# Reading w2 in whole 14 KiB runs in a DMA-bound decode kernel

## The chip, the cores and the metric

The kernel runs on one core of one Trainium2 chip. The metric is the device time of one execution in microseconds (us). Beside it each run lists the span of the core, from its first to its last instruction; the device time is longer than the span by some 2 us ("beyond the span" means device time minus span).

The names in the profiles: PE multiplies matrices (PEld loads its weights), DVE and ACT are the vector and the scalar engine, SP issues the large loads. A DMA is one such load; 16 DMA engines share its work. A load has landed when its last data have arrived in the on-chip memory. HBM is the large memory beside the chip's cores. A run of 14 KiB is a contiguous stretch of memory; a run of a kernel is one execution.

## The reference

One decode step for a batch of 4 with one token each, D = 1024. It is a pre-norm attention block with 32 query heads over 4 key/value heads (only the last 2048 of 8192 cached positions are used), followed by a gated feed-forward block with F = 3584, both with residuals. What matters here is its last line:

```python
gate = einsum("bsd,df->bsf", x, w1); up = einsum("bsd,df->bsf", x, w3)
h = silu(gate) * up
out = einsum("bsf,fd->bsd", h, w2)          # w2: (3584, 1024) bf16
```

With so few tokens the work is to read 55.6 MB of weights and caches once. w2 is 7.3 MB of that and is read last.

## The kernel before

All large loads go through one ring of ten buffers and are issued from SP in the order in which they are used: wq, k, v, wo, w1, w3, w2. Each is a chunk of about 2 MB. w2 is cut into JG = 4 chunks; in a chunk each of the 128 partitions takes IF = 7 consecutive rows of 2 KiB, 14 KiB that are contiguous in HBM.

```python
stream = ctx.enter_context(tc.tile_pool(name="stream", bufs=10))
w2_v = B_w2.rearrange("(j p i) n -> p j i n", p=P, i=IF)

def load_w2(j, pieces):
    w2_t = stream.tile([P, IF, D], BF16, tag="s")
    i = 0
    for n in pieces:                        # rows per DMA
        nc.sync.dma_start(out=w2_t[:, i : i + n, :], in_=w2_v[:, j, i : i + n, :])
        i += n
    return w2_t

plan = (
    # ... wq, k, v, wo, w1, w3 ...
    + [("w2", load_w2, (j, [4, 3] if j < JG - 1 else [3, 2, 1, 1])) for j in range(JG)]
)
```

The matmuls of a piece can start when its DMA has landed: four for each row i, one per quarter of the output columns.

```python
for jf in range(JG):
    w2_t = loaded["w2"][jf]
    for i in range(IF):
        for j in range(JG):
            nc.tensor.matmul(y2_ps[QD * j : QD * j + B, :], lhsT=hgT[:, i, jf, :],
                             rhs=w2_t[:, i, j * CG : (j + 1) * CG],
                             start=False, stop=(jf == JG - 1 and i == IF - 1),
                             skip_group_check=True)

res = act.tile([P, CG], BF16)
nc.vector.tensor_copy(out=res[:, : CG // 2], in_=y2_ps[:, : CG // 2])
nc.scalar.copy(out=res[:, CG // 2 :], in_=y2_ps[:, CG // 2 :])
# ... four small DMAs of res to the output, two on SP and two on ACT ...
```

## Time and profile before

| | before |
|---|---|
| device time, median of 3 runs | 140.01 us (139.9 to 140.39) |
| span of the profiled run | 138.2 us |
| data moved | 55.74 MB in 7025 DMA packets, 403 GB/s |
| busy: DMA engines / PE / DVE / ACT | 90% or more in slices 2 to 38 of 40 / 54% / 27% / 21% |

These are lines of the page of before: the engines' busy time and share of the span, the DMA engines' busy tenths and GB/s in 40 equal slices, the packets, and the shares of the chain that ended last.

```profile
span 138.2 us, 2365 instructions
PE 75.0 (54%) x1057; PEld 43.4 (31%) x1057; DVE 37.1 (27%) x71; ACT 29.4 (21%) x29; POOL 0.7 (1%) x6
...
DMA  5999999999999999999999999999999999999950
GB/s 154 433 423 436 417 436 436 441 413 432 441 402 409 420 421 416 425 423 430 429 429 417 425 442 424 428 432 428 432 428 432 432 432 413 421 427 430 409 216 2
DMA packets 7025, 55.74 MB, mean 403 GB/s; under 512 B 580, under 2 KB 612, under 8 KB 3560
...
DMA 74%; PE 16%; ACT 5%; SPq 1%; issue 1%; DVE 0%; ACTq 0%
```

The row of nines is the main reading: from the first microseconds to the last piece of w2 the DMA engines are busy 90% of the time or more, and no compute engine is busy for more than 54%. PE waits in the chain of k look like time (PE 16%), but the stream runs on below them.

The end of the same chain in order of time (start, duration, what) shows what stands behind the last landing:

```profile
121.33 12.97 DMA w_t<-in_B_w_dram
134.29 0.04 issue
134.34 0.41 PE y_ps L448 x4
134.75 0.02 issue
134.77 0.30 DVE res L458
135.07 0.02 issue
135.10 0.27 ACT res L459
```

Only four matmuls, two casts and the output DMA. The timeline of the w2 stage on PE (start, duration, engine, line, operation, count, and in brackets the idle time before it and what ended it):

```profile
121.20 1.66 PE L448 MATMUL y_ps<-w_t,hgT 128*4 128x256 bf16 x28 [0.31 <-DVE hgT L439]
123.84 1.02 PE L448 MATMUL y_ps<-w_t,hgT 128*4 128x256 bf16 x16 [0.97 <-DMA w_t<-in_B_w_dram]
...
125.68 0.81 PE L448 MATMUL y_ps<-w_t,hgT 128*4 128x256 bf16 x12 [0.82 <-DMA w_t<-in_B_w_dram]
...
128.11 1.02 PE L448 MATMUL y_ps<-w_t,hgT 128*4 128x256 bf16 x16 [1.61 <-DMA w_t<-in_B_w_dram]
...
133.08 1.00 PE L448 MATMUL y_ps<-w_t,hgT 128*4 128x256 bf16 x12 [0.42 <-DMA w_t<-in_B_w_dram]
...
134.34 0.38 PE L448 MATMUL y_ps<-w_t,hgT 128*4 128x256 bf16 x4 [0.25 <-DMA w_t<-in_B_w_dram]
```

PE is idle before every piece, and from the second chunk on the DMA ends the idle each time; before the first chunk, at 121.20 us, PE waited 0.31 us for DVE's copy of the transposed operand. The pieces come as the loads were cut: 16 and 12 matmuls for 4 and 3 rows. The tile view gives the issue times of the ten w2 DMAs on SP (count, duration in ns, first and last start in us):

```profile
L130 SPq DMA_DIRECT2D w_t<-in_B_w_dram x10: 328/328/328, 87.4 to 121.3; - x10
```

The last one is issued 13 us ahead of its landing.

Two readings come from the trace's packet records, one record for each packet. First, the duration of a packet by its size:

```
size     2 KiB   4 KiB   6 KiB   8 KiB   14 KiB   16 KiB   4 B (completion)
ns          84     159     234     309      535      611     9
```

That is 9 ns plus 37.6 ns per KiB (the prediction below says 36.6, a slip on which nothing else rests). Second, the 4-byte completion packets that each DMA engine writes at the end of its share show how the engines advance: 4.26 us per chunk of w1 or w3 (14 KiB runs), 4.30 to 4.31 us per chunk of w2. The bytes are the same.

### The profile page before, as it was taken

To read this page: it belongs to the slowest core of one execution; us is meant where nothing else is said; L and a number is where in the kernel's file an instruction comes from. 1 tells how busy PE (TensorE), PEld (TensorE's weight loads), DVE (VectorE), ACT (ScalarE), POOL (GpSimd) and SP (SyncE) were. 2 spreads that over 40 slices of the span, in tenths; PEclk is the share of its full clock that TensorE was granted. 3 is DMA by queue.
4 is the path that set the end of the run, shared out by engine and by line. 5 is a ranking of instruction groups with operands and counts; after the bars stand their busy time and mean duration, and the time that the engine had idled before them with its cause. 6 is when DMAs were issued, how large, how long until landed. Compare 5 with 4: busy or idle time off the path is not lost.

```text
span 138.2 us, 2365 instructions
## 1 busy us (share of the span) xinstructions
PE 75.0 (54%) x1057; PEld 43.4 (31%) x1057; DVE 37.1 (27%) x71; ACT 29.4 (21%) x29; POOL 0.7 (1%) x6
## 2 busy tenths in 40 slices
PE   0152254499798989300795489383244432663560
PEld 0111011295656556000795356131011110231220
DVE  6610000244343434520500460600008930300000
ACT  1200000126464646279420000000051000000000
POOL 2000000000000000000000000000000000000000
PEclk9999999999999999955555556855555555555555
DMA  5999999999999999999999999999999999999950
GB/s 154 433 423 436 417 436 436 441 413 432 441 402 409 420 421 416 425 423 430 429 429 417 425 442 424 428 432 428 432 428 432 432 432 413 421 427 430 409 216 2
DMA packets 7025, 55.74 MB, mean 403 GB/s; under 512 B 580, under 2 KB 612, under 8 KB 3560
## 3 DMA queue, kind: packets, MB, share of 16 engines
q1 hardware_dynamic: 6960, 55.58, 95.7%
q8 instruction: 8, 0.13, 0.3%
q10 hardware_dynamic: 56, 0.02, 0.1%
q14 instruction: 1, 0.01, 0.0%
HBM read 55.59 MB, written 0.01 MB: 402 GB/s over the span
## 4 chain that ended last, share of the span: by engine, by line
DMA 74%; PE 16%; ACT 5%; SPq 1%; issue 1%; DVE 0%; ACTq 0%
DMA w_t<-in_B_w_dram 55%; DMA k_t<-in_A_k_cache_dram 14%; PE kt_ps L271 10%; DMA wq_t<-in_A_wq_dram 5%; ACT kT L277 5%; PE scores_ps L256 5%; SPq L118 1%; PE y_ps L448 0%; DVE res L458 0%; ACT res L459 0%; SPq L111 0%; ACTq L277 0%
## 5 line engine op out<-in xcount | busy, mean ns | idle before, releaser
L277 ACT COPY kT<-kt_ps 128x1024 bf16<-128x1024 bf16 x16 | 15.9, 1013 | 14.5 <-PE kt_ps L271 14.5
L271 PE MATMUL kt_ps<-ident,k_t 128*128 128x128 bf16 x256 | 18.0, 231 | 0.9 <-DMA k_t<-in_A_k_cache_dram 0.9
L271 PEld LDWEIGHTS <-k_t 128*128 128x128 bf16 x256 | 15.9, 104 | 6.1 <-issue 4.9
L275 DVE COPY kT<-kt_ps 128x1024 bf16<-128x1024 bf16 x16 | 11.1, 692 | 17.6 <-PE kt_ps L271 17.6
L223 PE MATMUL q_ps<-wq_t,xnT 128*4 128x512 bf16 x64 | 7.5, 620 | 11.2 <-DMA wq_t<-in_A_wq_dram 11.2
L414 PE MATMUL u_ps<-w_t,hnT 128*4 128x448 bf16 x64 | 6.7, 567 | 10.3 <-DMA w_t<-in_B_w_dram 10.3
L256 PE MATMUL scores_ps<-kT,qz 128*32 128x512 bf16 x64 | 9.9, 609 | 3.0 <-ACT kT L277 3.0
L414 PEld LDWEIGHTS <-hnT 128*4 128x4 bf16 x128 | 3.9, 109 | 24.0 <-issue 23.4
L448 PE MATMUL y_ps<-w_t,hgT 128*4 128x256 bf16 x112 | 7.5, 404 | 6.3 <-DMA w_t<-in_B_w_dram 6.0
L414 PE MATMUL g_ps<-w_t,hnT 128*4 128x448 bf16 x64 | 6.5, 570 | 5.0 <-DMA w_t<-in_B_w_dram 4.7
L323 PE MATMUL OT_ps<-PT_sb,v_t 128*128 128x8 bf16 x256 | 7.4, 168 | 1.7 <-issue 1.4
L323 PEld LDWEIGHTS <-v_t 128*128 128x128 bf16 x256 | 7.3, 104 | 1.9 <-issue 1.7
L359 PE MATMUL y_ps<-wo_t,o_954 128*4 128x256 bf16 x128 | 6.4, 391 | 1.7 <-DVE y_ps L349 1.7
L223 PEld LDWEIGHTS <-xnT 128*4 128x4 bf16 x64 | 2.0, 106 | 15.8 <-issue 15.5
L309 PE MATMUL pt_ps<-Dm,Pm 128*128 128x128 bf16 x16 | 1.9, 308 | 9.3 <-DVE Dm L302 9.3
L459 ACT CAST res<-y_ps 128x128 bf16<-128x128 f32 x1 | 0.3, 267 | 31.0 <-DVE res L458 31.0
L448 PEld LDWEIGHTS <-hgT 128*4 128x4 bf16 x112 | 3.5, 103 | 10.3 <-issue 8.4
L427 DVE RECIPROCAL eg<-eg 128x896 f32<-128x896 f32 x1 | 5.8, 5753 | 0.0
L359 PEld LDWEIGHTS <-o_954 128*4 128x4 bf16 x128 | 4.0, 119 | 4.1 <-DVE y_ps L349 2.0
L233 DVE TENSOR_SCALAR q_sb<-q_ps 128x512 bf16<-128x512 f32 x1 | 0.7, 693 | 16.9 <-PE q_ps L223 16.9
L234 ACT ACTIVATE q_sb<-q_ps 128x512 bf16<-128x512 f32 x1 | 0.6, 597 | 20.9 <-DVE q_sb L233 20.9
L295 ACT ACTIVATE Pm<-scores_ps,nmax 128x2048 bf16<-128x2048 f32 x1 | 4.8, 4784 | 0.0
(73 smaller groups left out, 40.7 us busy)
## 6 DMA issues: line engine op xcount, KB each, us to landing
w_t<-in_B_w_dram SPq DMA_DIRECT2D x8, 1792.0 KB, 33.2
wq_t<-in_A_wq_dram SPq DMA_DIRECT2D x4, 2048.0 KB, 11.6
k_t<-in_A_k_cache_dram SPq DMA_DIRECT2D x4, 2048.0 KB
v_t<-in_A_v_cache_dram SPq DMA_DIRECT2D x4, 2048.0 KB, 40.4
wo_t<-in_A_wo_dram SPq DMA_DIRECT2D x4, 2048.0 KB
w_t<-in_B_w_dram SPq DMA_DIRECT2D x3, 1024.0 KB
w_t<-in_B_w_dram SPq DMA_DIRECT2D x4, 768.0 KB, 29.7
w_t<-in_B_w_dram SPq DMA_DIRECT2D x1, 512.0 KB
```

The costliest lines, as they stand in the source:

```text
L223: nc.tensor.matmul(q_ps[QD * g : QD * g + B, hf * 512 : (hf + 1) * 512], lhsT=xnT[:, kc, :], rhs=wq_t[:, kc % KPC, c0 : c0 + 512], start=( ...
L256: nc.tensor.matmul(scores_ps[QD * g : QD * (g + 1), n * 512 : (n + 1) * 512], lhsT=qz[:, b, g * QD : (g + 1) * QD], rhs=kT_v[:, g, :, :], ...
L271: nc.tensor.transpose(out=kt_ps[:, jj, :], in_=k_v[:, n * NJ + t * TB + jj, :], identity=ident[:])
L275: nc.vector.tensor_copy(out=kT[:, t * TB : (t + 1) * TB, :], in_=kt_ps[:])
L277: nc.scalar.copy(out=kT[:, t * TB : (t + 1) * TB, :], in_=kt_ps[:])
L295: nc.scalar.activation(out=Pm[:].rearrange("q (c jq) -> q jq c", jq=NSB), in_=scores_ps[:].rearrange("q (jq c) -> q jq c", jq=NSB), func=A ...
L309: nc.tensor.matmul(pt_ps[:, jj, :], lhsT=Pm[:, (jb * JPB + jj) * P : (jb * JPB + jj + 1) * P], rhs=Dm[:], start=True, stop=True)
L323: nc.tensor.matmul(OT_ps[:, b, g * REP : (g + 1) * REP], lhsT=v_t[:, g, j, :], rhs=PT_sb[:, j, g * QD + b * REP : g * QD + (b + 1) * REP], ...
L359: nc.tensor.matmul(y_ps[QD * j : QD * j + B, :], lhsT=o4[:, h4, r, :], rhs=wo_t[:, h4 % (HPC // RPO), r, j * CG : (j + 1) * CG], start=(h4 ...
L414: nc.tensor.matmul(out_ps[QD * j : QD * j + B, hf, :HF], lhsT=hnT[:, k2, r, :], rhs=w_t[:, r, c0 : c0 + HF], start=(k2 == 0 and r == 0), s ...
L427: nc.vector.reciprocal(out=eg[:], in_=eg[:])
L448: nc.tensor.matmul(y2_ps[QD * j : QD * j + B, :], lhsT=hgT[:, i, jf, :], rhs=w2_t[:, i, j * CG : (j + 1) * CG], start=False, stop=(jf == J ...
```

## The change

The intent is to spend fewer DMA packets and fewer DMAs on w2. The first three chunks are read in one DMA each, a 14 KiB run per partition. The last is cut into 4, 2 and 1 rows instead of 3, 2, 1 and 1.

```diff
-        + [("w2", load_w2, (j, [4, 3] if j < JG - 1 else [3, 2, 1, 1])) for j in range(JG)]
+        + [("w2", load_w2, (j, [IF] if j < JG - 1 else [4, 2, 1])) for j in range(JG)]
```

## The prediction

> **What bounds the kernel now.** The DMA stream. The profile page shows the 16 DMA engines 90% busy or more in slices 2 to 38 of 40, at 402 to 442 GB/s, while PE is busy 54% of the span, DVE 27%, ACT 21%. The chain of waits is 74% DMA and ends in three waits for w2 landings, the last at 134.29 us; after it stand only four matmuls (0.41 us), two casts (0.57 us) and the output DMA. The Trainium skill's page "DMA: Bandwidth & Descriptors" (section "Where 436 GB/s comes from") puts the ceiling at 435 GB/s, and most slices reach 417 to 435: only packet overhead is left to gain, since the change moves no bytes.
>
> **What it removes.** The trace's packet records give 84, 159, 234, 309, 535 and 611 ns for packets of 2, 4, 6, 8, 14 and 16 KiB: 9 ns plus 36.6 ns per KiB, and 9 ns for each 4-byte completion packet. The same page (section "Why small descriptors are slow (HBM only)") names a small fixed cost per packet; the 9 ns agree in kind. Each DMA engine carries 8 of 128 partitions, so per engine a chunk in pieces of 4 and 3 rows is 16 data packets and 2 completions, and as one run 8 and 1. The last chunk goes from 32 + 4 to 24 + 3. Each of the four chunks loses 9 packets: at 9 ns, 0.32 us in all. But successive packets overlap: one engine's completions are 4.26 us apart for a w1 or w3 chunk (14 KiB runs, same bytes) and 4.30 to 4.31 us for a w2 chunk. I take that measured 0.045 us per chunk: 4 x 0.045 = 0.18 us, all on the critical path.
>
> **What it adds or moves.** PE can start a chunk only when all of it has landed: 28 matmuls at once (1.66 us in this trace) in place of 16 and 12; that fits in the 4.3 us until the next. At the end the 4-row piece lands 1.9 us before the last row, its 16 matmuls take 1.02 us; the 2-row piece lands 0.68 us before it, its 8 matmuls issue in about 0.45 us. The last row leaves four matmuls exposed, as before. Six w2 DMAs in place of ten, with eight in flight: the last issues near 109 us instead of 121.3. It was already issued 13 us ahead of its landing, so this gains nothing. The other engines' streams stay the same.
>
> **Predicted time.** 140.01 - 0.18 = 139.8 us; 80% range 139.3 to 140.3, mostly run-to-run spread (139.9 to 140.39 before). Faster by over 2%: 0.01; within 2%: 0.98; slower: 0.01.
>
> **What would show it.** DMA packets fall by 576. One engine's completions in w2 come 4.26 us apart. The last matmul group starts near 134.15 us instead of 134.34, with PE idle about 0.2 us before it on the DMA. The y_ps matmuls have fewer and longer idles; their busy time stays near 7.5 us.
>
> **What would make it wrong.** 14 KiB packets running slower for w2 than for w1 and w3; the 2-row piece's matmuls still running when the last row lands (up to 0.2 us); or the eight DMA engines that now finish 1.3 us after the others (last packets end at 133.3 to 134.0 us against 132.2 to 132.6) falling further behind.

## The result, and the profile after

The changed kernel took 139.7 us (median of 6 runs, 139.59 to 139.9) against 140.41 us (139.9 to 140.51) for the six runs of before. The ratio is 0.996 with a 95% interval of 0.994 to 0.9979: within 2%, but clear of 1. A ratio is the mean time of one kernel's runs over that of the other's runs of the same rounds, so not quite the ratio of the quoted medians.

The same lines of the page of after:

```profile
span 137.7 us, 2361 instructions
...
DMA  5999999999999999999999999999999999999950
...
DMA packets 6449, 55.74 MB, mean 405 GB/s; under 512 B 516, under 2 KB 548, under 8 KB 2856
```

7025 - 6449 = 576 packets are gone, as counted beforehand, and the row of nines is unchanged. The end of the chain:

```profile
104.07 29.26 DMA w_t<-in_B_w_dram
133.33 0.04 issue
133.37 0.59 PE y_ps L448 x7
133.97 0.02 issue
133.98 0.41 PE y_ps L448 x4
134.39 0.02 issue
134.41 0.30 DVE res L458
134.72 0.02 issue
134.74 0.27 ACT res L459
```

The chain now leaves the DMA one piece earlier: it ends the wait for the 2-row piece, and the last four matmuls follow the earlier ones directly. The timeline of PE and the issue line of SP:

```profile
125.38 1.66 PE L448 MATMUL y_ps<-w_t,hgT 128*4 128x256 bf16 x28 [2.58 <-DMA w_t<-in_B_w_dram]
...
129.68 1.66 PE L448 MATMUL y_ps<-w_t,hgT 128*4 128x256 bf16 x28 [2.64 <-DMA w_t<-in_B_w_dram]
...
132.15 1.02 PE L448 MATMUL y_ps<-w_t,hgT 128*4 128x256 bf16 x16 [0.80 <-DMA w_t<-in_B_w_dram]
...
133.37 0.99 PE L448 MATMUL y_ps<-w_t,hgT 128*4 128x256 bf16 x12 [0.20 <-DMA w_t<-in_B_w_dram]
```

```profile
L130 SPq DMA_DIRECT2D w_t<-in_B_w_dram x6: 327/328/328, 87.1 to 108.3; - x6
```

Pieces of 28 matmuls have longer idles in front of them, still ended by the DMA. The packet records give what the DMA stream itself gained: from the last completion of w3 to the end of the last w2 data packet, which is called the w2 stage below, it took 134.00 - 116.69 = 17.31 us before and 133.65 - 116.52 = 17.13 us after. That is 0.18 us, the predicted amount. The windows view of these two stretches (stretch and its length, busy time of each engine, then PE clock, DMA share and GB/s) shows it as a rate, first before, then after:

```profile
116.70:134.00 17.30, 9.65 (x131) 4.45 (x131) 1.31 (x2) 0.00 (x0) 0.00 (x0) 0.50 0.96 398
```

```profile
116.50:133.65 17.15, 8.91 (x131) 4.65 (x131) 1.31 (x2) 0.00 (x0) 0.00 (x0) 0.50 0.95 403
```

But the time fell by more: 0.004 of 140.2 us is about 0.56 us, with an interval of 0.3 to 0.8. Some of the gain lies outside what the prediction had added up. The experiments look for it.

### The profile page after: what moved, and what is told of

Its sections match the earlier page's. It is cut to its first block, busy times and chain, and to the rows that moved or that the text cites. A ratio compares the mean times of both kernels' runs of the same rounds, so it can differ in the third digit from the quotient of the medians.

```text
span 137.7 us, 2361 instructions
## 1 busy us (share of the span) xinstructions
PE 73.3 (53%) x1057; PEld 43.4 (32%) x1057; DVE 37.0 (27%) x71; ACT 29.4 (21%) x29; POOL 0.7 (1%) x6
## 2 busy tenths in 40 slices
DMA packets 6449, 55.74 MB, mean 405 GB/s; under 512 B 516, under 2 KB 548, under 8 KB 2856
## 4 chain that ended last, share of the span: by engine, by line
DMA 61%; PE 22%; ACT 10%; DVE 2%; issue 2%; ACTq 0%
DMA w_t<-in_B_w_dram 42%; DMA k_t<-in_A_k_cache_dram 14%; PE kt_ps L271 11%; DMA wq_t<-in_A_wq_dram 5%; ACT kT L277 5%; PE scores_ps L256 5%; PE OT_ps L323 4%; ACT Pm L295 3%; DVE rmax L290 2%; PE pt_ps L309 1%; ACT L295 1%; PE y_ps L448 1%; ACT PT_sb L315 0%; DVE res L458 0%; ACT res L459 0%
## 5 line engine op out<-in xcount | busy, mean ns | idle before, releaser
L271 PE MATMUL kt_ps<-ident,k_t 128*128 128x128 bf16 x256 | 18.5, 235 | 0.9 <-DMA k_t<-in_A_k_cache_dram 0.9
L448 PE MATMUL y_ps<-w_t,hgT 128*4 128x256 bf16 x112 | 7.0, 410 | 6.7 <-DMA w_t<-in_B_w_dram 6.6
L359 PE MATMUL y_ps<-wo_t,o_954 128*4 128x256 bf16 x128 | 5.1, 337 | 1.7 <-DVE y_ps L349 1.7
L309 PEld LDWEIGHTS <-Pm 128*128 128x128 bf16 x16 | 1.6, 146 | 9.8 <-ACT Pm L295 9.8
```

Of the source, the lines that this page charges most:

```text
L271: nc.tensor.transpose(out=kt_ps[:, jj, :], in_=k_v[:, n * NJ + t * TB + jj, :], identity=ident[:])
L309: nc.tensor.matmul(pt_ps[:, jj, :], lhsT=Pm[:, (jb * JPB + jj) * P : (jb * JPB + jj + 1) * P], rhs=Dm[:], start=True, stop=True)
L359: nc.tensor.matmul(y_ps[QD * j : QD * j + B, :], lhsT=o4[:, h4, r, :], rhs=wo_t[:, h4 % (HPC // RPO), r, j * CG : (j + 1) * CG], start=(h4 ...
```

## The experiments

Theories at the start. *Packets*: each packet costs its engine about 5 ns beyond its bytes, and nothing else counts. *DMA count*: each DMA issued costs something of its own. *Tail*: how the last chunk is cut makes the gain. All kernels below gave the right result. The first four ran on one chip and share 11 runs of before (median 140.07 us); so do the next four among themselves (median 140.09 us).

### The changed kernel again

No edit. 

> The changed kernel again, to measure its gain closer. Packet theory (each packet costs about 5 ns of its engine's time beyond its bytes, 36 packets fewer per engine): 0.18 us faster than before, ratio 0.9987. Rival (each DMA issued costs something of its own, about 0.14 us, if the first measurement of 0.56 us was the whole effect of four DMAs fewer): 0.56 us faster, ratio 0.996.

Measured: 139.73 us (139.64 to 140.06), ratio 0.9967 (0.9948 to 0.9987), so about 0.46 us faster. The w2 stage in its trace took 17.13 us again. The packet theory's 0.9987 lies at the very edge of that interval, and the first measurement had left it outside. So the packets explain the stage but hardly the whole of the device time.

### Whole runs for the first three chunks only

```diff
-(j, [4, 3] if j < JG - 1 else [3, 2, 1, 1])
+(j, [IF] if j < JG - 1 else [3, 2, 1, 1])
```

> First three chunks in whole runs, last one still in pieces of 3, 2, 1, 1. Packet theory: 27 of the 36 packets go, 0.14 us faster than before. DMA-count theory: three of four DMAs go, 0.42 us faster. Tail theory (the gain comes from how the last chunk is cut): no change.

Measured: 139.73 us, ratio 0.9964 (0.9945 to 0.9982). The w2 stage took 17.18 us, 0.13 less than before: the packet theory's 0.14.

### The new cut of the last chunk only

```diff
-(j, [4, 3] if j < JG - 1 else [3, 2, 1, 1])
+(j, [4, 3] if j < JG - 1 else [4, 2, 1])
```

> First three chunks still 4 + 3, last one 4, 2, 1. Packet theory: 9 packets go, 0.05 us faster. DMA-count theory: 0.14 us faster. Tail theory: all of the gain, 0.4 to 0.6 us.

Measured: 139.9 us, ratio 0.9978 (0.996 to 0.9995). The w2 stage took 17.26 us, 0.05 less than before, as the packet theory has it. The tail theory, which wanted all of the gain here, is out: not by this time alone (0.07 to 0.56 us faster), but because the stage gained so little here and because whole_first3 gained 0.50 us with the old tail. A second thing stood out: all six runs lay between 139.88 and 139.94 us, while the 11 runs of before formed two groups, six at 139.96 to 140.07 and five at 140.29 to 140.68.

### Same DMAs, short runs

This keeps the six DMAs of after but deals the rows out differently, so that every run is one row of 2 KiB. The transposed operand follows suit, so the result stays right.

```diff
-    w2_v = B_w2.rearrange("(j p i) n -> p j i n", p=P, i=IF)
+    w2_v = B_w2.rearrange("(j i p) n -> p j i n", p=P, i=IF)
...
-    hg_v = hg[:].rearrange("q s c -> q (s c)").rearrange("q (p i) -> q i p", i=IF)
+    hg_v = hg[:].rearrange("q s c -> q (s c)").rearrange("q (i p) -> q i p", i=IF)
```

> Same six w2 DMAs as after, same bytes and same result, but w2's rows are dealt out so that every run is one row of 2 KiB: 56 data packets per engine and chunk in place of 8. Packet theory: an engine's completions in w2 come 4.54 us apart in place of 4.26 (84 ns per packet less 3 ns of overlap), w2 as a whole 1.0 us longer than after, so 0.85 us slower than before. DMA-count theory: same as after, so 0.2 to 0.6 us faster than before.

Measured: 140.58 us, ratio 1.0026 (1.0006 to 1.0045); spans of 138.6 to 139.0 us, mean 138.77, against 137.90 for after_again. One engine's completions came 4.48 to 4.49 us apart. From its page and from the windows view of its w2 stage:

```profile
DMA packets 9265, 55.74 MB, mean 401 GB/s; under 512 B 516, under 2 KB 548, under 8 KB 6184
```

```profile
116.80:134.77 17.97, 8.90 (x131) 4.63 (x131) 1.31 (x2) 0.00 (x0) 0.00 (x0) 0.50 1.00 386
```

The stage takes 17.96 us instead of 17.13 with the number of DMAs unchanged. That is 0.83 us for 176 more packets per engine (230 against 54), 4.7 ns each. The change itself saved 0.18 us with 36, 5.0 ns each. So the price of a packet holds over a lever five times as long, and the number of DMAs is not what moves the stage. Nor is it the new order of the rows in HBM: a 2 KiB packet took 84 ns here as in before.

### What lies beyond the span

The two groups of before are not a difference of its span. Device time minus span was 1.86 to 1.91 us in six of these 11 runs and 2.2 to 2.4 us in the other five; it was at most 1.91 us in all 30 runs of the other kernels so far (spans are listed to 0.1 us, so these differences are good to 0.05). Against the six quick runs alone (mean 140.00 us) the mean times of after_again, whole_first3 and last_only are 0.23, 0.30 and 0.09 us lower, where the packets ask for 0.18, 0.14 and 0.05. The packet records of the first profile of before, a run that took 2.4 us beyond its span, hold a packet that no other profile so far had:

```
queue 14 (instruction)   8192 B   start 140.28 us    (the span ended at 138.16)
```

The Trainium skill, "DMA: Bandwidth & Descriptors", section "Queues, rings and completion order", calls row 14 runtime-internal and names refill among its uses; the trace labels its packets "instruction", which agrees. Hence a fourth theory, *fetch*: with ten w2 DMAs the program of SP is just long enough to need one more block of instructions, and in some runs the end of the execution waits for it.

### Four more DMAs

The changed kernel, with four small loads of x on SP that nobody reads, so that SP issues 36 DMAs as before. The profile lists 67 SP instructions in both, and 63 in after.

```diff
     load_next(10)
+    spare = act.tile([B, JG, CG], BF16)
+    for j in range(JG):
+        nc.sync.dma_start(out=spare[:, j, :], in_=x_flat[:, j * CG : (j + 1) * CG])
```

> The changed kernel plus four 2 KiB loads of x into a tile nobody reads, put on SP early in the stream, so that SP issues as many DMAs as before. Fetch theory (5 of 11 runs of before took 2.2 to 2.4 us beyond the span of the core instead of 1.9, since SP's longer program makes it fetch 8 KiB of instructions once more after the end; the profile of before has such a packet at 140.3 us, the profiles of the other kernels have none): span as after, 137.9 us, but 2.2 to 2.4 us beyond it in some runs, and a late packet if the profile falls on such a run. Rival (the extra belongs to the 4 + 3 pieces, or to chance): always 1.8 to 1.9 us beyond the span, run time 139.7.

Measured: 139.92 us (139.72 to 140.3), ratio 0.9987 (0.9968 to 1.0006). Spans 137.8 to 138.0 us, mean 137.90, the same as after_again; the w2 stage 17.13 us. But two of the six runs took 2.32 and 2.40 us beyond the span. Four DMAs that have nothing to do with w2 brought the slow group back. The profiled run was of the quick group (1.87 us) and had no late packet; it had seven 8 KiB packets of queue 14 before the start, where the kernels with fewer DMAs have six.

### One row per DMA

```diff
-(j, [4, 3] if j < JG - 1 else [3, 2, 1, 1])
+(j, [1] * IF)
```

> Every w2 chunk in seven DMAs of one row: the 2 KiB packets of short_runs, but 28 w2 DMAs in place of 6. Packet theory at the 4.6 ns per packet that short_runs gave: 63 packets per engine and chunk, span 138.9 us, 0.1 us above short_runs. DMA-count theory (0.1 us or more for each DMA): 2 us or more above short_runs. Fetch theory: SP's extra fetch of instructions now falls into the run, so no run takes over 2.0 us beyond its span.

Measured: 141.25 us, ratio 1.0079 (1.0062 to 1.0096), mean span 139.43 us. That is 0.67 us above short_runs, neither the 0.1 of the packet theory nor the 2 of the DMA-count theory. The records place the difference. The last data packet ended at 134.81 us in this trace and at 134.77 in that of short_runs, and the w2 stage took 18.09 us against 17.96: 0.13 us for 22 more completions per engine, 5.9 ns each: about the packet price again, with no visible charge for the DMAs. The rest lies behind the stream: from the last completion of the output to the end of the span, 1.97 us against 1.39. In that stretch stands an 8 KiB packet of queue 14, at 139.26 us, 0.24 us before the end of the span. No run took over 2.0 us beyond the span (1.82 to 1.91), as the fetch theory said. But the span itself is longer, and the transfer of this packet is not the reason: SP's last waits were over 1.13 us after the last completion here (at 138.66 us) and 0.60 us after it in short_runs, so the time was lost before the packet started, and the packet ended 0.32 us after the span. Whether asking for the block cost SP the time, or something else did, was not tested.

### The last chunk whole too

```diff
-(j, [IF] if j < JG - 1 else [4, 2, 1])
+(j, [IF])
```

> The last chunk in one whole run too. If the prediction's account of the end holds, 28 matmuls (1.66 us) instead of four (0.4) stand behind the last landing, and 18 packets per engine fewer give back 0.1 us: span 139.0 us, 1.1 to 1.2 us above after. If packet count decided alone: 137.8 us.

Measured: 141.07 us, ratio 1.0064 (1.0048 to 1.008), mean span 139.27 us, 1.37 us above after_again. The timeline of its end:

```profile
134.38 1.66 PE L448 MATMUL y_ps<-w_t,hgT 128*4 128x256 bf16 x28 [2.92 <-DMA w_t<-in_B_w_dram]
...
136.09 0.29 DVE L458 CAST res<-y_ps 128x128 bf16<-128x128 f32 x1 [15.01 <-PE y_ps L448]
```

All 28 matmuls now stand behind the last landing, 1.66 us where 0.41 stood. The small pieces at the end are worth over ten times the packets they cost: 18 fewer per engine at 5 ns are 0.09 us. The measured loss is 0.2 us above the expected one; two pieces of it can be read. The end of the span, from the last completion of the output on, took 1.52 us against 1.40 in after_again. And the w2 stage of this trace took 17.29 us rather than the 17.05 that the packet count asks for. Its last landing, at 133.92 us, is that of a single engine, whose last chunk took 5.67 us (from 128.24) where the others took 4.26; the other 15 ended by 133.66, which would make 17.04. A 16 KiB instruction packet started at 129.31 us, within that chunk. More on these packets follows under "What could have made it wrong". The profiled run is the slowest of the six (141.38 us; the others took at most 141.19).

### One cast

Behind the last landing the result is cast by DVE and then, after DVE, by ACT. This takes one cast on DVE instead, on top of the change.

```diff
-    nc.vector.tensor_copy(out=res[:, : CG // 2], in_=y2_ps[:, : CG // 2])
-    nc.scalar.copy(out=res[:, CG // 2 :], in_=y2_ps[:, CG // 2 :])
+    nc.vector.tensor_copy(out=res[:], in_=y2_ps[:])
```

> The changed kernel with the result cast in one go on DVE in place of half on DVE and then half on ACT, which waits for DVE (0.29 + 0.03 + 0.27 us in the trace). One cast of 256 columns should take 0.29 + 128 columns at 0.96 per ns, 0.42 us: 0.17 us off the end, span 137.7 us, run 139.55. If the end were not on the critical path: as after.

Measured: 139.55 us (139.46 to 139.6), ratio 0.9955 (0.9939 to 0.9971), mean span 137.75 us. From the timeline:

```profile
134.58 0.42 DVE L458 CAST res<-y_ps 128x256 bf16<-128x256 f32 x1 [13.53 <-PE y_ps L448]
135.03 0.67 SPq L461 DMA_DIRECT2D out_dram<-res  x2
```

One cast of 0.42 us in place of 0.29 and 0.27 in a row. This is the fastest kernel measured. It beats before clearly; against the changed kernel the step is 0.15 us of span between kernels of two different submissions, and the intervals of the two ratios overlap. From the last data packet to the last completion of the output the trace has 2.62 us, against 2.67 in after and 2.72 in after_again, so the 0.17 us that the cast itself saved arrived only in part. One reason shows: the last four matmuls started 0.43 us after the last data packet here, 0.33 in after.

### Looks for the late packet

Two more profiles of the kernel before and one more of the one with four more DMAs, single runs.

> The kernel before once more, for its profile. Fetch theory: if the run takes 1.8 to 1.95 us beyond its span, the profile has no 8 KiB instruction packet after the span; if it takes over 2.1 us, it has one, as the first profile of before did (140.28 us, run 2.37 us beyond its span). Rival (the packet is always there and means nothing): a packet in either case. The w2 stage, from the last completion of w3 to the last data packet, 17.3 us in any case.

> As before_look1: late packet if and only if the run takes over 2.1 us beyond its span; w2 stage 17.3 us.

> As before_look1, for the changed kernel with four more small DMAs on SP (2 of its 6 runs took 2.3 to 2.4 us beyond the span, the profiled one 1.92 without a late packet): late packet if and only if the run takes over 2.1 us beyond its span; w2 stage 17.13 us.

Measured: all three fell on runs of the slow group, and all three have the packet.

| profile | SP DMAs | beyond the span, us | late 8 KiB packet at, us | w2 stage, us |
|---|---|---|---|---|
| before, first | 36 | 2.41 | 140.28 | 17.31 |
| before_look1 | 36 | 2.19 | 140.28 | 17.30 |
| before_look2 | 36 | 2.36 | 140.17 | 17.31 |
| four_more_look | 36 | 2.38 | 140.07 | 17.13 |
| four_more_dmas | 36 | 1.87 | none (one more before the start) | 17.13 |
| last_only | 35 | 1.86 | none | 17.26 |
| whole_first3 | 33 | 1.86 | none | 17.18 |
| after, after_again | 32 | 1.87, 1.85 | none | 17.13, 17.13 |
| short_runs | 32 | 1.86 | none | 17.96 |
| one_cast | 32 | 1.81 | none | 17.14 |
| all_whole | 30 | 1.86 | none | 17.29 |
| one_row_dmas | 54 | 1.85 | 139.26, inside the span | 18.09 |

The first four rows say more than that both occur together. The packets took 531, 324, 493 and 512 ns, and the runs 2.41, 2.19, 2.36 and 2.38 us beyond the span; but reckoned from the start of the span, the packet's end lies 0.24 us after the device time in all four. The end of the measured time moves with the end of this packet.

Over all timed runs with spans, before took over 2.1 us beyond the span in 8 of 22 and four_more_dmas in 2 of 6; the kernels with 35 SP DMAs or fewer in 0 of 42, and one_row_dmas with 54 in 0 of 6. The rival that the packet is always there falls, though all three profiles of before were slow, so that its quick runs were never looked into: a quick run with 36 SP DMAs was seen only in four_more_dmas. That the block belongs to SP's program is inferred from the count of SP's DMAs; no record names its owner. What decides in a given run whether the block is fetched ahead of the start or after the end stays open.

## Why the prediction was right, and where it fell short

- **The bound.** Right. The DMA engines stay at nine tenths in the same 37 slices in both profiles, and PE still waits for the DMA before every piece but the last. Of the prediction's three waits for "w2 landings" the first, up to 91.57 us, was for a load of w1, which has the same tile name. The 435 GB/s of the Trainium skill is its figure for the fabric; the same section puts the HBM side's limit for such loads at about 358 GB/s. This core moved 403 GB/s on average, and six slices read 436 to 442, so the trace shows neither figure as a hard limit.
- **The packets.** Right in count (576) and in price. The w2 stage fell from 17.31 to 17.13 us, 0.18 as predicted; the halves of the change gave 0.13 and 0.05. The price measured between successive completions was the right one to use: the raw 9 ns of a packet record would have given 0.32 us, since records overlap by about 3 to 4 ns.
- **Completions 4.26 us apart.** Right: 119.14, 123.40 and 127.66 us for the first engine of a group in the trace of after.
- **PE and the end.** Right in effect. The last group of matmuls started at 133.98 us instead of 134.15, since the whole stream of that run was 0.17 us early (w3's last completion at 116.52 against 116.69 us). The idle of 0.2 us before it did not appear: the 2-row piece's matmuls took 0.59 us up to the last four, not the estimated 0.45. The last four still started 0.33 us after the last data packet, as before (0.34), so it cost nothing here, but the cut 4, 2, 1 has no slack left; in one_cast, with the same cut, they started 0.43 us after it. Busy time of the y_ps matmuls was 7.0 us rather than 7.5.
- **Earlier issue gains nothing.** Right for the stream: the last w2 DMA was issued at 108.3 us instead of 121.3.
- **What could have made it wrong.** None of it occurred in the trace of after: 14 KiB packets of w2 took 535 ns like those of w1 and w3, and the late DMA engines ended 1.3 us after the others as before. What makes them late can be read from the record. Up to the end of w3 every one of the 13 profiles has eight instruction packets during the run (seven of 16 KiB and one of 8 KiB, at 31, 43, 54, 59, 73, 79, 85 and 99 us in before), and after each of them one more engine completes its share late: of the 16 engines, 15 are on time after the first packet and 8 after the eighth. That is a match of times, not an experiment.
- **The size of the gain.** Too small. That the predicted 139.8 us was met so closely is partly luck, beside the wide range: the 140.01 us it started from, the median of three runs, was by its time a quick run, and quick runs are all that the changed kernel has. Six runs of before had a median of 140.41, from which the same step would have led to 140.23. "140.01 - 0.18" took the gain of the stream for the gain of the kernel. In the rounds of after_again the mean device time fell by 0.43 us. Of that 0.20 us lies beyond the span (2.07 us on average for before, 1.87 for after_again) and 0.24 us within it (138.14 against 137.90). The first part is the extra instruction fetch that four DMAs fewer on SP avoid; four_more_dmas restored it with w2 untouched. The second is the 0.18 us of the packets and about 0.06 us that stay open: the end of the span, from the last completion of the output on, took 1.49 to 1.51 us in the five profiles with 36 SP DMAs and 1.39 to 1.40 in the four with 32, but 1.52 in all_whole with 30, so no rule can be read from it. The step of the prediction that fell short is therefore "mostly run-to-run spread (139.9 to 140.39 before)": that spread was not noise but two groups of runs, and the change removed the slower one.

## What to carry to other kernels

When the DMA engines are busy from end to end, count packets: a run split in two costs each engine about 5 ns per packet, so 14 KiB against 2 KiB runs is 5% of a stage's time, and 14 KiB against 8 + 6 KiB is 1%. Cut only the last chunk small, so that little compute stands behind the last landing; that was worth 1.3 to 1.4 us here, while the cut itself cost under 0.1. When a kernel's runs fall into two groups, subtract the span before calling it noise: a cause outside the span, here one fetch of instructions, can be worth as much as the change under study.

## What the Trainium skill lacked or had wrong

- "DMA: Bandwidth & Descriptors", section "Why small descriptors are slow (HBM only)", gives a fixed overhead of about 3 cycles per packet, but no time for contiguous runs of kilobytes, which is what the profile counts as packets. In a stream that hardly rests the runs show 4.7 to 5.0 ns for each: at 2 KiB against 14 KiB, 0.83 us of a 17.1 us stage.
- The same page, section "Measured (HBM→SBUF, 128 partitions, SWDGE, issued from GpSimd)", advises batches of 1 MiB and more. With eight DMAs in flight from SP, 28 DMAs of 256 KiB took 18.09 us for 7.34 MB, 406 GB/s, against 17.96 us for six DMAs with the same 2 KiB packets. The page has no figure for DMAs that are queued behind others, where the size of a DMA hardly counted here.
- "Runtime: NRT & Kernel Launch", section "Instruction fetch mechanics", calls the cost of crossing a 16 KiB block of instructions "mostly hidden". That speaks of the engine that runs the program; what the fetch does to loads that keep the DMA engines busy is missing. Every profile here has eight 16 KiB instruction packets during the run, of 0.88 to 0.97 us each, and one of 8 KiB. After the first of them, at 31 us, one DMA engine falls behind (before: its completion at 33.28 us, those of the other 15 engines between 31.55 and 31.98), and each further one is followed by one more late engine; by the end nine of 16 run 1.3 us behind the others in before and after, and the last landing waits for them. That is read from the traces and was not tested by an experiment.
- The same section does not say that a fetch can fall behind the end of the program. Here an 8 KiB one there went with 0.3 to 0.5 us more device time, in 10 of 28 timed runs of the kernels with 36 SP DMAs and in none of 42 with 35 or fewer.
